# Transposing exp(C) and A by DMA instead of on TensorE, from the third batch on

## The chip, the cores and the metric

The kernel runs on one core of a Trainium2 chip. The metric is the device time of one execution in microseconds (us). Five engines work side by side, each through its own list of instructions in order: TensorE (PE; its weight loads are shown apart as PEld), VectorE (DVE), ScalarE (ACT), GpSimd (POOL) and SyncE (SP). POOL and SP also issue transfers, which 16 DMA engines carry out. Semaphores tie the lists together.

## The reference, cut to what matters

There are 8 batches of 8 heads, with 576 rows of 64 values each for q, k and v. First comes a Nystrom attention with 32 landmarks per head, then an MLP over all 4608 tokens:

```
q_lm = q.reshape(B, H, 32, 18, 64).mean(axis=3);  k_lm likewise
A = softmax(q @ k_lm.T / 8)       # 576 x 32 per head
Bm = softmax(q_lm @ k_lm.T / 8)   # 32 x 32
C = softmax(q_lm @ k.T / 8)       # 32 x 576
Z = Bm.T / (norm1(Bm) * norminf(Bm) + 1e-6)
for _ in range(6): Z = 2 * Z - Z @ Bm @ Z
x = A @ Z @ C @ v                 # heads side by side: 4608 x 512
h = x @ w_in                      # 4608 x 2048
out = (h * sigmoid(h)) @ w_out    # 4608 x 512
```

C is contracted with v over the 576 keys, so exp(C) is needed with the keys on the partitions; the scores come out of TensorE with (head, landmark) on the partitions. A comes out with the tokens on the partitions and is needed with (head, landmark) there. Both have to be transposed.

## The kernel before

Each batch passes through an attention stage and an MLP stage. The eight heads form two groups g of four, so that 4 heads by 32 landmarks fill 128 partitions.

Attention stage of a batch (class `Att`):

- `c_scores(g)` (L288) computes the scores of C for a group into a pair of PSUM banks, 128 x 576. `c_max` (L296) takes the row maximum on DVE. `c_exp(g)` (L304) is one ACT instruction with a running sum that writes a contiguous 128 x 576 bf16 tile `eC`.
- `c_transpose(g)` (L311) is six PE transposes of 128 x 96 pieces. Piece c takes every sixth column of `eC`, since v is loaded with key 6n + c at partition n. They go to one PSUM tile, `ctp`. `c_out(g)` (L317) copies it to `eCT` in SBUF: on DVE for batches 1 to 7, on ACT for batch 0.
- `w_mm(g)` (L328) multiplies `eCT` with v in 24 small matmuls (`wp`), and `w_out` (L337) scales the result by `wsc`, which `w_scale` (L322) prepares on DVE.
- `a_scores`, `a_max`, `a_shift` and `a_exp` produce exp(A) in three parts of 256, 256 and 64 tokens. `a_norm(i)` (L408) sums and inverts on DVE (L412, L413) and multiplies on POOL (L414) into `an`.
- `a_transpose(g)` (L418) is five PE transposes into the PSUM tile `atp`, `a_out(g)` (L425) a DVE copy into `AT`.
- `b_*`, `f_mm`, `f_out`, `ns_mm` and `ns_step` compute Z: a PE product (`fi`) and a DVE step (`fx`, L281) alternate six times. `x_out`, `z_mm` and `m_unit` fold Z, C v and w_in into `mb`.

MLP stage: `l1_mm` (L448) is four matmuls of `mb` with `AT` per step (`hps`) and `l1_act` (L458) the Silu on ACT. `l2_mm(n)` (L468) issues the next n matmuls with w_out (`ops`). After every 16, ACT copies the bank to `ost` (L484, three buffers) and SP issues its store (L486). `ops` has one PSUM bank; `hps` and the scores of C share two pairs of banks.

The order is written out by hand. Loop b (L570) runs 16 steps s of the MLP of batch b and puts the attention of batch b + 1 between them. With d = 0 (d = 4 in loop 0): step d+1 has the scores of B and C(0); d+2 the other scores and all exponentials, between two loads of an ACT table; d+3 `c_transpose(0)`, `f_mm`, `f_out`, `c_out(0)`; d+4 `c_transpose(1)`, `a_norm(0)`, `c_out(1)`, `w_scale`, `a_norm(1)`; d+5 `w_mm(0)`, `a_norm(2)`; d+6 `w_mm(1)`; d+7 and d+8 `a_transpose` and `a_out` of the groups. Steps d+3 to d+8 end with an `ns_mm`. The batch whose attention is worked on in loops 1 to 6 is thus batch 2 to 7; batch 0's stands ahead of the loops and batch 1's in loop 0. The lists EVEN and ODD (L489) say how many matmuls with w_out go into each step of an even or odd loop.

POOL issues all loads (L91 for q and k of batch b + 3, L98 for v of batch b + 2). SP issues the 36 stores and nothing else. Tiles wait for one another through semaphores that the framework places; tiles with one buffer (`an`, `eC`, `eCT`) are written again only when the readers before have ended.

Of the kernel before, what the change touches and what calls it, by code (L numbers as in the profile page):

```python
# [9 lines left out]
BF = mybir.dt.bfloat16  # L10
AF = mybir.ActivationFunctionType
# [24 lines left out]
def kernel(  # L36
# [9 lines left out]
    nc = tc.nc  # L46
    B, H, S, Dh = q.shape
    L = 32
    SEG = S // L
# [3 lines left out]
    sc = 1.0 / float(Dh) ** 0.5  # L53
    HF = S // 2
    VP = 96
    VC = S // VP
    TCH = [(c, min(c + 128, S)) for c in range(0, S, 128)]

    constp = ctx.enter_context(tc.tile_pool(name="constp", bufs=1))
    loadp = ctx.enter_context(tc.tile_pool(name="loadp", bufs=2))  # L60
    attp = ctx.enter_context(tc.tile_pool(name="attp", bufs=2))
# [8 lines left out]
    def mm(o, lhsT, rhs, start, stop):  # L70
        nc.tensor.matmul(out=o, lhsT=lhsT, rhs=rhs, start=start, stop=stop,  # L71
                         skip_group_check=True)
# [4 lines left out]
    def ps1(nm, dt=FP):  # L77
        return psa.tile([128, 512 if dt == FP else 1024], dt, tag="a", name=nm)
# [32 lines left out]
    for j in range(4):  # L111
        nc.gpsimd.dma_start(
            out=w_out_sb[:, 4 * j:4 * j + 4, :],
            in_=moe_w_out[512 * j:512 * j + 512, :].rearrange("(c p) m -> p c m", p=128))
# [11 lines left out]
    for i in range(2):  # L126
        z = constp.tile([128, 4, 4 * L, 2], BF, tag=f"bd{i}", name=f"bd{i}")
        nc.vector.memset(z, 0.0)
        bd_t.append(z)
    mask = constp.tile([128, 4, L], BF, tag="mask", name="mask")  # L130
    nc.vector.memset(mask, 0.0)
    for h in range(4):
        nc.vector.memset(mask[32 * h:32 * h + 32, h, :], 1.0)
    ident = constp.tile([128, 128], BF, tag="ident", name="ident")
# [43 lines left out]
    class Att:  # L178
        def __init__(self, b):
            self.b = b  # L180
            self.qkT, self.v, self.lmn = qkT_t[b], v_t[b], lmn_t[b]
            self.bd = bd_t[b % 2]
            self.lmk = attp.tile([128, 2, L, 2], BF, tag="lmk", name="lmk")
            self.csum = attp.tile([128, 2], FP, tag="csum", name="csum")
            self.eC, self.eCT, self.t = [None, None], [None, None], [None, None]
            self.s, self.sa, self.w = [None, None], [None] * 3, [None, None]
            self.fx = None

# [107 lines left out]
        def c_max(self, g):  # L296
# [4 lines left out]
            nc.vector.tensor_scalar(out=bs, in0=mx, scalar1=sc / SEG, scalar2=None, op0=OP.mult)  # L301
            self.t[g] = bs

        def c_exp(self, g):  # L304
            e = attp.tile([128, S], BF, tag=f"eC{g}", name="eC", bufs=1)
            nc.scalar.activation(out=e.rearrange("p (a n) -> p a n", a=2),  # L306
                                 in_=self.s[g][:, :, 0:HF], func=AF.Exp, scale=sc / SEG,
                                 bias=self.t[g], accum_out=self.csum[:, g:g + 1])
            self.eC[g] = e

        def c_transpose(self, g):  # L311
            self.t[g] = ps1("ctp", BF)
            for c in range(VC):
                nc.tensor.transpose(self.t[g][0:VP, 128 * c:128 * c + 128],  # L314
                                    self.eC[g].rearrange("p (n c) -> p c n", c=VC)[:, c, :], ident)

        def c_out(self, g, copy=nc.vector.tensor_copy):  # L317
            e = attp.tile([VP, VC, 128], BF, tag=f"eCT{g}", name="eCT", bufs=1)
            copy(out=e.rearrange("p c n -> p (c n)"), in_=self.t[g][0:VP, 0:VC * 128])
            self.eCT[g] = e  # L320

        def w_scale(self):  # L322
            self.wsc = attp.tile([128, 2], FP, tag="wsc", name="wsc")
# [4 lines left out]
        def w_mm(self, g):  # L328
            vv = self.v.rearrange("p h (c d) -> p h c d", d=Dh)
            self.w[g] = ps1("wp")  # L330
            for c in range(VC):
                for h in range(4):
                    mm(self.w[g][32 * h:32 * h + 32, 0:Dh],
                       self.eCT[g][:, c, 32 * h:32 * h + 32], vv[:, 4 * g + h, c, :],
                       start=(c == 0), stop=(c == VC - 1))

        def w_out(self, g):  # L337
# [70 lines left out]
        def a_norm(self, i):  # L408
            c, n, pr = self.a_dims(i)
            x = self.ex[0:pr, c:c + n, :].rearrange("p c (h l) -> p (c h) l", l=L)  # L410
            r = self.arec[0:pr, c:c + n, :].rearrange("p c h -> p (c h)")
            nc.vector.tensor_reduce(out=r, in_=x, op=OP.add, axis=AX.X)  # L412
            nc.vector.reciprocal(out=r, in_=r)  # L413
            nc.gpsimd.tensor_tensor(  # L414
                out=self.an[0:pr, c:c + n, :].rearrange("p c (h l) -> p (c h) l", l=L), in0=x,
                in1=r.unsqueeze(2).to_broadcast((pr, 8 * n, L)), op=OP.mult)

        def a_transpose(self, g):  # L418
            self.at = ps1("atp", BF)
            for (c, (c0, c1)) in enumerate(TCH):  # L420
                pr = c1 - c0
                nc.tensor.transpose(self.at[:, c0:c1], self.an[0:pr, c, 128 * g:128 * g + 128],  # L422
                                    ident[0:pr, 0:pr])

        def a_out(self, g):  # L425
            nc.vector.tensor_copy(out=self.AT[:, g, :], in_=self.at[:, 0:S])


        def m_unit(self, f):
# [69 lines left out]
    a = Att(0)  # L499
# [70 lines left out]
    for b in range(B):  # L570
        nxt = b + 1 < B
        cnt = EVEN if b % 2 == 0 else ODD
        h = {}
        a0 = a
        a = Att(b + 1) if nxt and b else None
# [9 lines left out]
        for s in range(NDC):  # L585
            if b == 0 and s < 4:
# [8 lines left out]
                else:  # L595
                    landmarks_out(1, lp, 0, 4)
                    a = Att(1)
# [113 lines left out]
        n = 4 + b % 2  # L711
# [32 lines left out]
```

## Time and profile before

| | |
|---|---|
| median of three runs | 315.83 us (314.72 to 316.62) |
| the profiled execution's own time | 316.06 us |
| its span, first to last instruction | 314.1 us, so 1.96 us lie around it |
| PE / DVE / ACT / POOL busy | 284.4 / 178.1 / 173.8 / 118.3 us |
| mean granted TensorE clock | 0.982 |
| `ctp` transposes of exp(C): 96 matmuls, mean | 290 ns each, weight loads 224 ns |
| `atp` transposes of A: 80 matmuls | 233 ns (64 of them) and 204 ns (16) each, weight loads 104 and 94 ns |

Matmuls overlap, so a mean duration of one is longer than the time by which it moves the next. The chain of work shows the time that each adds: it follows the last instruction back to what released it, and its pieces lie end to end.

### The profile page before, as it was taken

To read this page: it belongs to the slowest core of one execution; us is meant where nothing else is said; L and a number is where in the kernel's file an instruction comes from. 1 tells how busy PE (TensorE), PEld (TensorE's weight loads), DVE (VectorE), ACT (ScalarE), POOL (GpSimd) and SP (SyncE) were. 2 spreads that over 40 slices of the span, in tenths; PEclk is the share of its full clock that TensorE was granted. 3 is DMA by queue.
4 is the path that set the end of the run, shared out by engine and by line. 5 is a ranking of instruction groups with operands and counts; after the bars stand their busy time and mean duration, and the time that the engine had idled before them with its cause. 6 is when DMAs were issued, how large, how long until landed. Compare 5 with 4: busy or idle time off the path is not lost.

```text
span 314.1 us, 6108 instructions
## 1 busy us (share of the span) xinstructions
PE 284.4 (91%) x2472; PEld 164.0 (52%) x2472; DVE 178.1 (57%) x429; ACT 173.8 (55%) x337; POOL 118.3 (38%) x141
## 2 busy tenths in 40 slices
PE   2666967789999999999999999999999999999995
PEld 2453645435654665466546564466546654555442
DVE  4775788766677665756695567566676633000000
ACT  1225496448556854667467745685578546446311
POOL 7234322990397029540892079203950110100000
PEclk9999999859999999999999999999999999999999
DMA  6999997517064616055438224000600110010121
GB/s 119 209 212 206 198 212 139 77 21 154 20 104 89 137 60 111 33 97 123 78 66 146 74 56 90 33 33 35 112 33 35 61 39 36 35 67 33 57 78 67
DMA packets 18780, 28.17 MB, mean 90 GB/s; under 512 B 1345, under 2 KB 9537, under 8 KB 18753
## 3 DMA queue, kind: packets, MB, share of 16 engines
q0 software_dynamic: 13568, 18.35, 35.3%
q1 hardware_dynamic: 5184, 9.44, 8.1%
q8 instruction: 19, 0.31, 0.4%
q14 instruction: 9, 0.07, 0.1%
HBM read 36.70 MB, written 9.44 MB: 147 GB/s over the span
## 4 chain that ended last, share of the span: by engine, by line
PE 81%; DVE 9%; ACT 4%; DMA 2%; issue 2%; POOL 1%; ACTq 0%; POOLq 0%
PE ops L71 42%; PE hps L71 18%; PE sa L71 5%; PE mp L71 4%; PE ctp L314 3%; ACT ost L484 2%; DMA nat<-in_q_dram 2%; PE fi L71 2%; PE scp L71 2%; DVE qkT L142 2%; PE atp L422 2%; PE wp L71 1%; DVE cmx L298 1%; PE lmp L71 1%; DVE arec L412 1%
## 5 line engine op out<-in xcount | busy, mean ns | idle before, releaser
L71 PE MATMUL ops<-w_out_sb,gT 128*128 128x512 bf16 x576 | 147.0, 382 | 2.4 <-ACT ost L484 2.0
L460 ACT ACTIVATE gT<-hps 128x576 bf16<-128x576 f32 x128 | 82.3, 650 | 81.2 <-PE hps L71 81.0
L71 PE MATMUL hps<-AT,mb 128*128 128x288 bf16 x512 | 85.4, 293 | 0.0
L71 PEld LDWEIGHTS <-gT 128*128 128x128 bf16 x576 | 51.3, 99 | 53.3 <-issue 10.7
L71 PEld LDWEIGHTS <-mb 128*128 128x128 bf16 x512 | 48.4, 100 | 25.4 <-issue 2.5
L414 POOL TENSOR_TENSOR an<-ex,arec 128x512 bf16<-128x512 bf16 (+1 forms) x24 | 21.4, 905 | 100.1 <-DVE arec L413 91.5
L142 DVE STREAM_TRANSPOSE qkT<-nat 128x576 f32<-128x576 f32 x32 | 39.8, 1243 | 1.6 <-DMA nat<-in_k_dram 1.2
L484 ACT COPY ost<-ops 128x512 f32<-128x512 f32 x36 | 21.1, 585 | 27.4 <-PE ops L71 24.6
L439 DVE CAST mb<-mp 128x512 bf16<-128x512 f32 x32 | 22.0, 688 | 15.3 <-PE mp L71 15.3
L281 DVE SCALAR_TENSOR_TENSOR fx<-fx,fi 128x320 bf16<-128x320 bf16 (+1 forms) x48 | 20.4, 424 | 16.6 <-PE fi L71 16.6
L164 POOL TENSOR_TENSOR lma<-nat 128x1152 f32<-128x1152 bf16 x12 | 28.5, 2375 | 0.0
L440 ACT CAST mb<-mp 128x512 bf16<-128x512 f32 x32 | 18.6, 582 | 4.6 <-PE mp L71 4.6
L121 ACT ACT_TABLE_LOAD x16 | 20.5, 1283 | 1.1 <-PEq L728 0.8
L71 PE MATMUL fi<-fx 128*128 128x160 bf16 (+1 forms) x96 | 14.9, 240 | 4.8 <-DVE fx L281 3.0
L71 PEld LDWEIGHTS <-fx 128*128 128x128 bf16 x96 | 8.3, 102 | 17.7 <-DVE fx L281 7.0
L71 PE MATMUL mp<-w_in_sb,zwT 64*32 64x512 bf16 x256 | 14.9, 418 | 2.6 <-ACT mb L440 1.4
L392 DVE TENSOR_REDUCE nm<-sa 128x16 bf16<-128x512 f32 (+1 forms) x24 | 13.7, 594 | 5.3 <-PE sa L71 5.1
L71 PEld LDWEIGHTS <-ident 128*128 128x128 bf16 x168 | 10.0, 118 | 12.1 <-issue 5.0
L405 ACT ACTIVATE ex<-sa 128x512 bf16<-128x512 f32 (+1 forms) x24 | 12.5, 524 | 5.5 <-PE sa L71 5.5
L314 PEld LDWEIGHTS <-eC 128*96 128x96 bf16 x96 | 14.5, 224 | 1.5 <-issue 0.5
L314 PE MATMUL ctp<-ident,eC 128*96 128x128 bf16 x96 | 14.3, 290 | 0.4 <-ACT ex L405 0.4
L306 ACT ACTIVATE eC<-scp,cbs 128x576 bf16<-128x576 f32 x16 | 11.7, 740 | 4.4 <-DVE cbs L301 4.2
(68 smaller groups left out, 287.1 us busy)
## 6 DMA issues: line engine op xcount, KB each, us to landing
out_dram<-ost SPq DMA_DIRECT2D x36, 256.0 KB, 2.0
nat<-in_k_dram POOLq DMA_DIRECT2D x16, 288.0 KB, 6.6
nat<-in_q_dram POOLq DMA_DIRECT2D x16, 288.0 KB, 8.1
v<-in_v_dram POOLq DMA_DIRECT2D x8, 576.0 KB, 6.3
w_in_sb<-in_moe_w_in_dram POOLq DMA_DIRECT2D x4, 512.0 KB, 13.6
w_out_sb<-in_moe_w_out_dram POOLq DMA_DIRECT2D x4, 512.0 KB, 16.3
```

The source lines that it names most:

```text
L71: nc.tensor.matmul(out=o, lhsT=lhsT, rhs=rhs, start=start, stop=stop, skip_group_check=True)
L121: nc.scalar.activation(out=spare[:, 1:2], in_=spare[:, 0:1], func=func)
L142: nc.vector.transpose(out=o.rearrange("p (l t) -> p t l", t=SEG), in_=nat_t[b][:, j, :].bitcast(FP).rearrange("p (t l) -> p t l", l=L))
L164: nc.gpsimd.tensor_tensor(out=a1, in0=nat[:, :, 0:3 * w], in1=nat[:, :, 3 * w:6 * w], op=OP.add)
L281: nc.vector.scalar_tensor_tensor(out=n[:, :, lo:160], in0=self.fx[:, :, lo:160], scalar=2.0, in1=self.p.rearrange("p (g n) -> p g n", g=2) ...
L314: nc.tensor.transpose(self.t[g][0:VP, 128 * c:128 * c + 128], self.eC[g].rearrange("p (n c) -> p c n", c=VC)[:, c, :], ident)
L392: nc.vector.tensor_reduce(out=self.nm[0:pr, c:c + n, :], in_=self.sa[i][0:pr, 0:256 * n].rearrange("p (c h l) -> p c h l", h=8, l=L), op=O ...
L414: nc.gpsimd.tensor_tensor(out=self.an[0:pr, c:c + n, :].rearrange("p c (h l) -> p (c h) l", l=L), in0=x, in1=r.unsqueeze(2).to_broadcast(( ...
L439: nc.vector.tensor_copy(out=o[:, 0, :], in_=m[0])
L440: nc.scalar.copy(out=o[:, 1, :], in_=m[1])
L460: nc.scalar.activation(out=gT_t[b][:, dc, o:o + S].rearrange("p (a n) -> p a n", a=2), in_=h[:, :, 0:HF], func=AF.Silu)
L484: nc.scalar.copy(out=ost, in_=st["ps"])
```

## The change

- Two constant tiles `eC_t[g]`, 128 x 6 x 128 bf16, replace `eC`; the last 32 columns of each 128 are set to zero once at the start.
- `c_exp(g)` writes its 576 values in chunk order in all batches: ACT reads PSUM with a step of six values and writes runs of 48. The PE transposes that remain (batches 0 and 1) read contiguous pieces.
- For batches 2 to 7 `c_transpose` and `c_out` do nothing. Instead `c_exp(g)` is followed by one transposing DMA on SP's queue, from `eC_t[g]` (128 x 768) to `eCT[g]` (128 x 6 x 128).
- For batches 2 to 7 `a_transpose` and `a_out` do nothing. Instead each `a_norm` is followed by a transposing DMA on SP for each chunk of 128 tokens (64 for the last): five per batch, from `an` to `AT`.

```diff
+    eC_t = []
+    for g in range(2):
+        z = constp.tile([128, VC, 128], BF, tag=f"eC{g}", name=f"eC{g}")
+        nc.vector.memset(z[:, :, VP:128], 0.0)
+        eC_t.append(z)
...
+            self.by_dma = b >= 2
...
         def c_exp(self, g):
-            e = attp.tile([128, S], BF, tag=f"eC{g}", name="eC", bufs=1)
-            nc.scalar.activation(out=e.rearrange("p (a n) -> p a n", a=2),
-                                 in_=self.s[g][:, :, 0:HF], func=AF.Exp, scale=sc / SEG,
-                                 bias=self.t[g], accum_out=self.csum[:, g:g + 1])
-            self.eC[g] = e
+            nc.scalar.activation(
+                out=eC_t[g][:, :, 0:VP].rearrange("p c (a n) -> p a c n", a=2),
+                in_=self.s[g][:, :, 0:HF].rearrange("p a (n c) -> p a c n", c=VC), func=AF.Exp,
+                scale=sc / SEG, bias=self.t[g], accum_out=self.csum[:, g:g + 1])
+            self.eCT[g] = attp.tile([128, VC, 128], BF, tag=f"eCT{g}", name="eCT", bufs=1)
+            if self.by_dma:
+                nc.sync.dma_start(out=self.eCT[g], in_=eC_t[g].rearrange("p c n -> p (c n)"),
+                                  transpose=True)
 
         def c_transpose(self, g):
-            self.t[g] = ps1("ctp", BF)
-            for c in range(VC):
-                nc.tensor.transpose(self.t[g][0:VP, 128 * c:128 * c + 128],
-                                    self.eC[g].rearrange("p (n c) -> p c n", c=VC)[:, c, :], ident)
+            if not self.by_dma:
+                self.t[g] = ps1("ctp", BF)
+                for c in range(VC):
+                    nc.tensor.transpose(self.t[g][0:VP, 128 * c:128 * c + 128],
+                                        eC_t[g][:, c, 0:VP], ident)
 
         def c_out(self, g, copy=nc.vector.tensor_copy):
-            e = attp.tile([VP, VC, 128], BF, tag=f"eCT{g}", name="eCT", bufs=1)
-            copy(out=e.rearrange("p c n -> p (c n)"), in_=self.t[g][0:VP, 0:VC * 128])
-            self.eCT[g] = e
+            if not self.by_dma:
+                copy(out=self.eCT[g][0:VP].rearrange("p c n -> p (c n)"),
+                     in_=self.t[g][0:VP, 0:VC * 128])
...
-                       self.eCT[g][:, c, 32 * h:32 * h + 32], vv[:, 4 * g + h, c, :],
+                       self.eCT[g][0:VP, c, 32 * h:32 * h + 32], vv[:, 4 * g + h, c, :],
...
+            if self.by_dma:
+                for m in range(c, c + n):
+                    c0, c1 = TCH[m]
+                    nc.sync.dma_start(out=self.AT[:, :, c0:c1], in_=self.an[0:pr, m, :],
+                                      transpose=True)
 
         def a_transpose(self, g):
+            if self.by_dma:
+                return
             self.at = ps1("atp", BF)
...
         def a_out(self, g):
-            nc.vector.tensor_copy(out=self.AT[:, g, :], in_=self.at[:, 0:S])
+            if not self.by_dma:
+                nc.vector.tensor_copy(out=self.AT[:, g, :], in_=self.at[:, 0:S])
```

More of the change, by code (lines that the diff above doesn't have):

```diff
@@ L184, in __init__ @@
             self.csum = attp.tile([128, 2], FP, tag="csum", name="csum")
-            self.eC, self.eCT, self.t = [None, None], [None, None], [None, None]
+            self.eCT, self.t = [None, None], [None, None]
+            self.by_dma = b >= 2
             self.s, self.sa, self.w = [None, None], [None] * 3, [None, None]
```

## The prediction

> **What bounds the kernel now.** I read the page's busy times and slices first, then the chain of work, over the span and over one loop, then the order of events on each engine around what is changed, and last the DMA share there.
>
> ```profile
> PE 284.4 (91%) x2472; PEld 164.0 (52%) x2472; DVE 178.1 (57%) x429; ACT 173.8 (55%) x337; POOL 118.3 (38%) x141
> PE   2666967789999999999999999999999999999995
> PE 81%; DVE 9%; ACT 4%; DMA 2%; issue 2%; POOL 1%; ACTq 0%; POOLq 0%
> ```
>
> From the tenth slice (about 70 us) PE never pauses: what leaves PE's list there shortens the run, unless a wait fills the place. The chain through loop 3 (the MLP of batch 3 with the attention of batch 4) gives the time that each piece of PE adds:
>
> ```profile
> 146.11 0.72 PE ctp L314 x6
> 146.83 0.12 PE f L71 x2
> ...
> 147.46 0.31 PE fi L71 x2
> 147.78 0.49 PE hps L71 x4
> 148.27 0.73 PE ctp L314 x6
> ...
> 154.15 0.35 PE atp L422 x5
> ...
> 155.89 0.35 PE atp L422 x5
> ```
>
> The four groups that the change takes off PE are all on the chain: 0.72 + 0.73 + 0.35 + 0.35 us. The chain of loop 2 shows the same (0.72, 0.73, 0.35, 0.36). In order of time, the same loop:
>
> ```profile
> 141.24 0.20 ACT L306 ACTIVATION_READ_ACCUMULATOR eC<-scp,cbs 128x1 f32 x1
> 141.95 0.21 ACT L306 ACTIVATION_READ_ACCUMULATOR eC<-scp,cbs 128x1 f32 x1
> 146.15 1.17 ACT L460 ACTIVATE gT<-hps 128x576 bf16<-128x576 f32 x2
> 149.34 1.04 POOL L414 TENSOR_TENSOR an<-ex,arec 128x512 bf16<-128x512 bf16 x1 [10.98 <-DVE arec L413]
> 149.69 0.70 DVE L325 TENSOR_TENSOR wsc<-wsc,nrm 128x2 f32<-128x2 f32 x1
> 150.42 0.36 PE L71 MATMUL wp<-v,eCT 96*32 96x64 bf16 x24
> 151.68 0.11 PEld L71 LDWEIGHTS <-fx 128*128 128x128 bf16 x2 [0.43 <-DVE fx L281]
> 152.41 0.36 PE L71 MATMUL wp<-v,eCT 96*32 96x64 bf16 x24
> ```
>
> exp(C) of the groups ends at 141.44 and 142.16 and is first used by `w_mm` at 150.42 and 152.41: that gap must cover a transposing DMA. At 151.68 PE's weight load already waits for DVE.
>
> **Part 1: transposes off PE (batches 2 to 7).** 6 x (0.72 + 0.73 + 0.35 + 0.35) = 12.9 us, from the chain. The DVE copies that go with them (two `eCT` of 0.52, two `AT` of 0.46) are off the chain.
>
> **Part 2: what is late next.** Between the `fi` of step d+3 and that of d+5, DVE runs one `ns_step`, `a_norm(0)`, `c_out(1)`, `w_scale`, `a_norm(1)` and the next `ns_step`: from 147.81 to 151.62. PE is only 0.43 behind in that weight load (about 0.1 in the chain: `fi` takes 0.25 there against 0.14 elsewhere). PE loses 0.73 of work there. DVE loses `c_out(1)`, 0.49, but the `wsc` product after it ends at 150.39, when POOL's product (149.34 + 1.04) ends; that `wsc` takes 0.70 in these batches and 0.16 at its shortest, so it is held beside POOL. If it is held until POOL ends again, DVE gains nothing and PE gives back 0.73 - 0.1 = 0.63. If it slips in ahead of POOL, DVE gains about 0.9 and nothing is given back. POOL starts 0.16 after the reciprocal that both follow, the time of the `wsc` reciprocal, so held is nearer: I take 0.5 per batch, 3.0 us in all, ends 0 and 3.8. At the `fi` products of steps d+4 and d+6 to d+8 DVE is done 0.6 us or more before PE comes (154.19 against 154.88 at step d+7), which covers the 0.35 removed there.
>
> **Part 3: exponentials in chunk order.** No row has ACT reading PSUM with a step. Bounds: nothing, or 576 elements at half rate, +0.58 each (0.74 less some 0.16 of fixed time). In loops 1, 3 and 5 `hps` of step d+4 needs the banks that the Silu starting at 146.15 frees at 146.80; PE comes at 147.61, and 0.72 earlier after the change: 0.09 us later than the bank. ACT has pauses of 0.45 and 0.16 before that, so 2 x 0.58 would cost about 0.5 in each of three loops, and about 1.2 each in batches 0 and 1: 3.9 us. Nearest is the contiguous row with as many elements; I take nothing. In batches 0 and 1 the weight loads of 128x96 (224 ns, stepping by six) become contiguous, towards the 104 ns of `an`. Their 24 products add 10.4 - 6 x 1.45 = 1.7 us to the chain (3.3% of the span, less part 1's). At the pace of the A transposes (0.07 us each for 0.12) that saves 0.7; with nothing gained from layout, 0. I take 0.4. The two fills of zeros lie under the first load (DMA until 10.24 us); their nearest row, the `bd` fill, takes 0.49.
>
> **Part 4: the transposing DMAs.** The trace has none. Seven join 4.5 stores per batch on SP, at 0.33 us of issue each for the stores: 2.3 us of SP per batch, which has room in 31.8 to 35.3. Low bound of one: a 256 KB store lands in 2.0 us. High bound: the load of v, 768 pieces of 1.5 KB, as many as the 128 x 6 rows of 256 B in exp(C), lands in 6.3 us, 4.3 of them moving. The need: `w_mm(0)` moves to about 149.0 and `w_mm(1)` to 151.0, so 7.5 us after the first exponential (8.1 in even loops) and 8.8 after the second (9.4). At the low bound, one behind the other, the second lands in 4. At the high bound the second lands 9.9 after its exponential: 1.1 and 0.5 late, 5 us over six batches. The loads of q and k share the engines until about 145.5, and in loops 1 to 4 until 76, 109, 145.5 and 174:
>
> ```profile
> 140.00:142.00 2.00, 2.00 (x23) 1.21 (x21) 1.96 (x4) 2.00 (x9) 0.00 (x0) 1.00 1.10 225
> 144.00:146.00 2.00, 2.00 (x14) 1.25 (x13) 0.53 (x4) 1.98 (x3) 0.00 (x0) 1.00 0.73 200
> 146.00:148.00 2.00, 1.91 (x17) 1.35 (x16) 1.02 (x3) 1.31 (x4) 0.00 (x0) 1.00 0.02 8
> out_dram<-ost SPq DMA_DIRECT2D x36, 256.0 KB, 2.0
> v<-in_v_dram POOLq DMA_DIRECT2D x8, 576.0 KB, 6.3
> ```
>
> (Ahead of the last two columns, DMA share and GB/s, stand the engines and the clock; then follow the issues, ended by us to landing.) The slowest store took 6.4 us. Even that delay leaves the pair inside the window if each then moves like a store. exp(C) is 192 KB per DMA, less than a store's 256: I take the store's side, no stall.
>
> The five DMAs for A start when POOL ends (150.4 and 153.0) and are first read by the next loop's `hps` (167.35, some 1.7 earlier after the change): 12 us for 1152 rows, 6.5 us at v's rate. Stores queue on SP behind POOL's products through these DMAs, by about a microsecond; three `ost` buffers cover it, at one store per 7 us.
>
> The Trainium skill, "DMA: Bandwidth & Descriptors" (Latency and other measured facts), gives a transposing DMA 261 GB/s when it isn't contiguous, and about 2.0 us fixed (Anatomy of one DMA); as an estimate 2.8 us for one of exp(C), which is hidden, so the sum would stand. The same page's Rules for kernel authors speak against the change: transfers under 64 KB pay mostly overhead, and A goes in pieces of 64 and 32 KB. By five times those 2.0 us one after another A lands some 10 us after POOL, still inside the window, and the sum again stands.
>
> **The sum**, against the profiled execution's own 316.06 (span 314.1; the median of the runs is 0.23 lower): 316.06 - 12.9 + 3.0 - 0.4 = 305.8 us.
>
> **Rivals.**
>
> *Late transposes, slower.* Place: the two `w_mm` of each batch, PE waiting on DMA. It loses 1 us per batch for each us that the second DMA lands beyond 8.8 (9.4) after its exponential. The net saving is 10.3 / 6 = 1.7 per batch, so it turns slower at about 10.8. For it: v's rate (9.9), with loads on the same engines in four of six batches adding 2 to 4: 2 x 0.8 + 4 x 3.8 = 17 us, giving 323. At twice v's price the pair needs 19.2 from the first issue, 9.7 late: 305.8 + 58 = 364. Against it: as few bytes as a store, which lands in 2.0.
>
> *Late transposes, part of the gain left.* v's rate without harm from the loads: 305.8 + 5 = 311.
>
> *SP becomes the serial part.* If each transposing DMA holds SP until it has moved, seven must fit beside 4.5 stores in 31.6 us less 10: it decides from (31.6 - 10 - 1.5) / 7 = 2.9 us each. Below that only stores wait. At 4.3 us each, loops would stretch by 7 x (4.3 - 2.9) = 10 us, 365. Against it: the store's 0.33 us of issue.
>
> *ACT sets the pace.* Stepped reads at half rate: 305.8 + 3.9 = 309.7. For it: the 0.09 us of margin in odd loops. Against: the margin is 1 us or more in even loops (d+3 holds four more matmuls).
>
> *No change.* The DMAs are issued and PE's list is shorter in any case; the time could stay within 0.5% only where a stall of about 1.7 per batch cancels the saving.
>
> **How the numbers follow.** 0.5%, 1.6 us, is about what a measurement of this kernel can tell from no change. Hidden, as summed, ACT's rival included: 0.57, with its own range 301.5 (0 for part 2, 0.7 for batches 0 and 1, and 0.3% between runs) to 309.7. Partly late, to 314.2: 0.09. Cancelled, 314.3 to 317.4: 0.05. Slower to 332, by late transposes beside loads: 0.16. Beyond, by twice v's price or by SP: 0.13. Faster 0.66, same 0.05, slower 0.29. The range runs from 301.5 to 330, which leaves out the last case and a little of both ends.
>
> **What would show it.** Right: PE's share unbroken from 70 to 255 us; no `ctp` or `atp` in the chain but for batches 0 and 1; the DMAs of exp(C) landing within 7 us; PE's wait for `fx` at step d+5 grown to about 0.9. Wrong: PE or its weight loads waiting on a DMA into `eCT` ahead of `wp` or into `AT` ahead of `hps`; stores late on SP with ACT waiting for `ost`; `eC` activations well over 0.74. The prediction fails above all if a transposing DMA takes more than 5 us of its queue.

## The result and the profile after

The changed kernel takes 299.97 us (median of 4 runs, 298.71 to 300.45) against 315.27 (4 runs): a ratio of 0.950, 95% interval 0.946 to 0.955. A second comparison gave 299.81 against 315.62, 0.948 (0.944 to 0.952). The prediction was 305.8, with a range from 301.5 to 330. The direction held, and so did the removal of four groups of transposes from PE's chain; the gain was half as large again, above all because a loss of 3.0 us that the prediction counted, for a product on DVE held up beside POOL's, did not come. The profiled execution took 300.44 with a span of 298.7, so the span shrank by 15.4 us.

The page of the changed kernel first: busy times, PE by slices, the row of the exponentials, and the new issues (count, then median us from issue to landing):

```profile
PE 266.3 (89%) x2305; PEld 150.7 (50%) x2340; DVE 165.8 (55%) x407; ACT 174.2 (58%) x337; POOL 118.2 (40%) x141
PE   1766886769999999999999999999999999999994
L314 ACT ACTIVATE eC<-scp,cbs 128x576 bf16<-128x576 f32 x16 | 11.7, 741 | 4.8 <-DVE cbs L309 4.7
AT<-an SPq DMA_TRANSPOSE x30, 4.3
eCT<-eC SPq DMA_TRANSPOSE x12, 3.7
```

PE is still unbroken from about 67 us on. It is busy for 18 us less, up to 6 of which are records that this trace lacks: 2305 matmuls stand beside 2340 weight loads, and the 35 are `ops`, busy for 141.1 us and not 147.0. Reading PSUM with a step of six cost ACT nothing: 741 ns against 740. The transposing DMAs land inside their windows: the slowest of exp(C) takes 6.3 us, and the first `w_mm` comes 7.5 us after the first exponential.

The order of time in loop 3, the loop that the prediction was worked out on:

```profile
136.12 2.69 SPq L320 DMA_TRANSPOSE eCT<-eC  x2
143.03 0.11 DVE L337 RECIPROCAL wsc<-csum 128x2 f32<-128x2 f32 x1
143.17 0.16 DVE L338 TENSOR_TENSOR wsc<-wsc,nrm 128x2 f32<-128x2 f32 x1
143.25 2.72 POOL L427 TENSOR_TENSOR an<-ex,arec 128x512 bf16<-128x512 bf16 x3 [10.24 <-ACT gT L481]
143.62 0.36 PE L71 MATMUL wp<-v,eCT 96*32 96x64 bf16 x24
144.62 0.27 PEld L71 LDWEIGHTS <-fx 128*128 128x128 bf16 x2 [0.17 <-DVE fx L289]
145.50 0.36 PE L71 MATMUL wp<-v,eCT 96*32 96x64 bf16 x24
```

The DMAs of exp(C) are issued at 136.12 and are not waited for at 143.62 and 145.50. The `wsc` product starts 0.08 us before POOL's and takes 0.16; before, it started 0.35 after POOL and took 0.70. PE's wait for `fx` went from 0.43 to 0.17 where the prediction had it grow to 0.9. And the chain of the same loop, from step d+3 to step d+8:

```profile
139.47 1.29 PE ops L71 x6
140.76 0.13 PE f L71 x2
...
141.71 0.49 PE hps L71 x4
142.20 0.86 PE ops L71 x4
143.06 0.14 PE fi L71 x2
...
143.69 0.29 PE wp L71 x24
143.98 0.16 issue
144.14 0.81 PE ops L71 x3
144.95 0.14 PE fi L71 x2
...
146.76 0.49 PE hps L71 x4
147.25 0.65 PE ops L71 x3
...
148.52 0.05 issue
148.57 0.59 PE ops L71 x2
```

The four groups are gone, and 0.32 more per loop. `fi` at step d+5 takes 0.14 instead of 0.25. The three `ops` of steps d+7 and d+8, which stood behind the transposes of A, add 0.65 and 0.05 + 0.59 instead of 0.75 each. From one store copy to the same one a loop later, loop 3 went from 31.77 to 29.28, which is 2.49; 2.15 + 0.11 + 0.2 accounts for it.

Counted from the start of the first exponential of C in one batch to that in the next, the 15.4 us come from these stretches: 1.2 before that of batch 2 (73.59, now 72.38); 1.7 in loop 1; 2.5 in each of loops 2 to 5 (for example 35.25 to 32.78 and 31.77 to 29.29); 2.6 from there to the end.

### The profile page after: what moved, and what is told of

Same layout as the page of the kernel before. It is cut to its first block, busy times and chain, and to the rows that moved or that the text cites. A ratio compares the mean times of both kernels' runs of the same rounds, so it can differ in the third digit from the quotient of the medians.

```text
span 298.7 us, 5888 instructions
## 1 busy us (share of the span) xinstructions
PE 266.3 (89%) x2305; PEld 150.7 (50%) x2340; DVE 165.8 (55%) x407; ACT 174.2 (58%) x337; POOL 118.2 (40%) x141
## 4 chain that ended last, share of the span: by engine, by line
PE 79%; DVE 9%; ACT 4%; issue 3%; DMA 2%; POOL 1%; ACTq 0%; POOLq 0%
PE ops L71 43%; PE hps L71 19%; PE sa L71 5%; PE mp L71 4%; ACT ost L505 3%; PE scp L71 2%; DMA nat<-in_q_dram 2%; DVE qkT L148 2%; PE fi L71 2%; PE wp L71 1%; PE lmp L71 1%; DVE cmx L306 1%; DVE arec L425 1%; DVE fx L289 1%; DVE fx L274 1%
## 5 line engine op out<-in xcount | busy, mean ns | idle before, releaser
L71 PE MATMUL ops<-w_out_sb,gT 128*128 128x512 bf16 x541 | 141.1, 382 | 5.3 <-ACT ost L505 2.0
L71 PEld LDWEIGHTS <-gT 128*128 128x128 bf16 x576 | 52.2, 98 | 54.2 <-issue 11.3
L306 DVE TENSOR_REDUCE cmx<-scp 128x1 f32<-128x576 f32 x16 | 12.1, 755 | 4.0 <-PE scp L71 3.5
L71 PE MATMUL lmp<-nat,ident 128*128 128x64 bf16 x144 | 8.2, 229 | 6.7 <-DMA nat<-in_k_dram 5.6
```

The source lines that it names most:

```text
L306: nc.vector.tensor_reduce(out=mx, in_=self.s[g][:, :, 0:HF], op=OP.max, axis=AX.XY, negate=True)
```

## The experiments

Times are medians; ratios are to the kernel before on the same chip.

**Chunk order alone** (`e1_chunk_only`): which part of the gain needs no DMA?

```diff
-            self.by_dma = b >= 2
+            self.by_dma = False
```

> Exponentials in chunk order in all batches, all transposes on PE. Theory: part of the gain needs no DMA. In the changed kernel the six transposes of batch 1 that read contiguous pieces add 0.34 us to the chain where they added 0.73, so batches 2 to 7 would save 6 x 2 x 0.39 = 4.6 and batches 0 and 1 the 1.2 already seen; the wsc product stays held beside POOL, since the copy of eCT ahead of it remains, and may give back up to 0.3 per batch. 309.5 to 311.5. Rival, as in the prediction: layout is worth only 0.4, the rest is the DMA's: 314.5 to 315.5.

313.14 us, ratio 0.991 (0.988 to 0.994): 2.5 us of gain, more than the prediction's 0.4 and less than the theory's 4 to 6. The chain of this kernel in loop 3 shows where the rest stayed:

```profile
144.49 0.34 PE ctp L327 x6
...
145.46 0.33 PE fi L71 x2
...
145.81 0.49 DVE fx L289
146.30 0.60 DVE arec L425
...
146.93 0.25 DVE arec L426
147.18 0.41 DVE eCT L332
147.59 0.08 DVE wsc L337
...
147.69 0.70 DVE wsc L338
148.39 0.61 DVE arec L425
...
149.02 0.25 DVE arec L426
149.27 0.36 DVE fx L289
...
149.68 0.31 PE fi L71 x2
```

A group of six transposes does add 0.34 now, not 0.72. But with PE shorter, the chain leaves PE between the two `fi` products and runs through DVE: the very row of instructions that the prediction's part 2 listed, with the held `wsc` product of 0.70 and the copy of `eCT` in it. Loops 2 to 5 shrank by 0.38 or 0.39 each (31.77 to 31.38), half of the 0.77 that the two groups lost.

**Chunk order alone, `wsc` first** (`e9_chunk_wsc_first`): is it the held product?

```diff
-                    a.c_out(1)
-                    a.w_scale()
+                    a.w_scale()
+                    a.c_out(1)
```

> Chunk order alone (all transposes on PE), with w_scale moved ahead of the copy of eCT at step d+4, no DMA transposes. Theory: in the run with chunk order alone the wsc product was held (0.70) and DVE's row of instructions up to fx set the pace at step d+5, so of 0.77 per loop only 0.38 came through. With w_scale first the product starts before POOL, takes 0.16, DVE is 0.54 earlier and PE gets the rest: 6 x 0.4 to 0.5 less than chunk order alone, 310 to 311. Rival, the bank copies or ACT hold PE there: 313, no change.

308.94 us, ratio 0.977 (0.974 to 0.981), 1 us below the range expected. All eight `wsc` products take 0.16, and loops 2 to 5 take 34.37 and 30.87, 0.5 less than with chunk order alone. Moving one small instruction in the list was worth about 4 us by the medians (3.0 between the spans of the two profiled executions, 311.0 and 308.0), and it needs none of the DMAs.

**exp(C) by DMA, A on PE** (`e2_c_dma_only`). The flag of `c_exp`, `c_transpose` and `c_out` stays, that of `a_norm`, `a_transpose` and `a_out` becomes false.

```diff
-            self.by_dma = b >= 2
+            self.c_dma = b >= 2
+            self.a_dma = False
```

> Batches 2 to 7: exp(C) by DMA, A transposed on PE as before. Theory: the A transposes are on the chain, 0.70 per batch, and lengthen the matmuls around them by 0.2 (the three ops behind them take 0.75 in the chain, without them 0.65): 6 x 0.9 = 5.4 over the changed kernel, 305.4. Rival, PE has slack that other waits fill once exp(C) is gone: within 2 us of the changed kernel, 300 to 302.

305.26 us, ratio 0.966 (0.961 to 0.971). Theory: the loops take 33.70 and 30.21, 0.92 more than in the changed kernel, for the 0.70 of the transposes and the 0.2 around them.

**A by DMA, exp(C) on PE** (`e3_a_dma_only`).

```diff
+            self.c_dma = False
+            self.a_dma = b >= 2
```

> Batches 2 to 7: A by DMA, exp(C) in chunk order transposed on PE and copied by DVE. Theory: the transposes cost 2 x 0.34 per batch on the chain, and with the copy of eCT back ahead of it the wsc product is held beside POOL again, which costs PE 0.1 to 0.5 at the fi product of step d+5: 6 x (0.68 + 0.1 to 0.5) = 4.7 to 7.1 over the changed kernel, 304.7 to 307. Rival, the wsc product isn't held: 304.

307.05 us, ratio 0.972 (0.967 to 0.976): theory, at its upper end. The `wsc` product is held again (median 0.69), and the chain runs through DVE as in the run above. The kernel itself, in the same comparison:

> The changed kernel itself, beside the kernel before and the parts on one chip. All theories: about 300, ratio 0.950.

So, counted from chunk order alone (313.1), exp(C) by DMA brings 7.9, A by DMA 6.1, both together 13.3.

**A DVE instruction in place of the copy** (`e4_dve_fill`): the changed kernel, with a sum over 384 columns whose result nobody reads.

```diff
+                scr = attp.tile([128, 12], FP, tag="scr", name="scr")
+                nc.vector.tensor_reduce(
+                    out=scr, in_=self.ex[:, 0:2, :].rearrange("p c (h l) -> p (c h) l", l=L)[:, 0:12, :],
+                    op=OP.add, axis=AX.X)
...
                     a.c_out(1)
+                    a.dve_fill()
                     a.w_scale()
```

> The changed kernel with one more DVE instruction (a sum over 384 columns, about 0.5 us, result unused) where the copy of eCT stood, ahead of w_scale, in batches 2 to 7. Theory: the prediction's part 2 failed because without that copy the wsc product starts 0.06 us after the reciprocal and POOL only 0.14 after it, so it gets in first; with 0.5 us ahead of it POOL is first again, wsc takes 0.70 instead of 0.16, DVE is 1.0 later, and PE waits about 1.1 at the fi product of step d+5, 0.8 of it on the chain: 6 x 0.8 = 5 over the changed kernel, 305. Rival, wsc was short for another reason (its reciprocal takes 0.11 now, not 0.15): wsc stays at 0.16, DVE is 0.5 later, 6 x 0.3 = 2, 302.

304.83 us, ratio 0.968 (0.963 to 0.972), at the theory's 305. In order of time, loop 3:

```profile
143.09 0.49 DVE L338 TENSOR_REDUCE scr<-ex 128x12 f32<-128x384 bf16 x1
143.32 1.04 POOL L434 TENSOR_TENSOR an<-ex,arec 128x512 bf16<-128x512 bf16 x1 [10.24 <-ACT gT L488]
...
143.69 0.69 DVE L345 TENSOR_TENSOR wsc<-wsc,nrm 128x2 f32<-128x2 f32 x1
145.66 0.11 PEld L71 LDWEIGHTS <-fx 128*128 128x128 bf16 x2 [1.15 <-DVE fx L289]
```

With half a microsecond ahead of it the product meets POOL's, is held to about POOL's end (143.32 + 1.04), and PE waits 1.15. The loops take 0.82 more each. Of the 1.05 by which the product ends later than in the changed kernel (144.38 against 143.33), the sum itself explains at most 0.49. This is the state that the prediction assumed for the changed kernel.

**Late transposes, made true** (`e6_six_more`): three unused transposing DMAs of exp(C) ahead of each of the two real ones.

```diff
             if self.by_dma:
+                for i in range(3):
+                    more = attp.tile([128, VC, 128], BF, tag=f"more{g}{i}", name="more", bufs=1)
+                    nc.sync.dma_start(out=more, in_=eC_t[g].rearrange("p c n -> p (c n)"),
+                                      transpose=True)
```

> The changed kernel with three more transposing DMAs of exp(C), into unused tiles, ahead of each of the two real ones. Theory: each holds SP for 1.24 us, one behind the other, and lands some 2.5 after its hold ends; the second real one then lands 8 x 1.24 + 2.5 = 12.4 after the first issue, where w_mm of group 1 stands 9.4 (odd loops) to 10 after it: PE waits 2.4 to 3 per batch, 6 x 2.7 = 16 over the changed kernel, 316. This is the prediction's rival of late transposes, made true. If SP's hold overlaps with the next DMA (no queueing): below 302. If loads slow them further in four of six batches: 320 to 325.

348.14 us, ratio 1.104 (1.100 to 1.108). The sign is right, the price far off: 48 us over the changed kernel and not 16. From the order of time in loop 2 (SP, POOL's load of v, PE):

```profile
124.10 0.85 POOL L98 DMA_DIRECT2D v<-in_v_dram  x1
124.41 1.25 SPq L324 DMA_TRANSPOSE eCT<-eC  x1
126.39 5.87 SPq L437 DMA_TRANSPOSE AT<-an  x4
132.69 0.51 PE L71 MATMUL wp<-v,eCT 96*32 96x64 bf16 x24 [8.79 <-DMA eCT<-eC]
133.13 1.89 PE L71 MATMUL ops<-w_out_sb,gT 128*128 128x512 bf16 x4
```

The issues do queue as expected, but the last one goes out just behind the load of v and takes 8.2 us to land, where the median is 2.8. Then PE, after 8.8 us of waiting, runs at half the clock: four `ops` take 1.89 and not 1.03. Over the whole run PE waits 36.7 us for `eCT`, more than twice the 16 expected. By stretches of the same loop (PE, PEld, DVE, ACT and POOL busy, then the granted clock, DMA share, GB/s):

```profile
123.00:127.00 4.00, 0.89 (x8) 0.43 (x5) 0.74 (x3) 0.65 (x1) 3.99 (x4) 1.00 0.78 116
127.00:131.00 4.00, 0.00 (x0) 0.00 (x0) 0.00 (x0) 0.00 (x0) 3.69 (x6) 0.52 1.23 178
131.00:135.00 4.00, 2.31 (x30) 1.12 (x31) 0.00 (x0) 0.31 (x1) 3.83 (x3) 0.50 0.91 206
135.00:139.00 4.00, 4.00 (x21) 2.19 (x19) 0.97 (x2) 1.25 (x2) 0.91 (x2) 0.70 0.00 0
```

**The same with v's load later** (`e12_six_more_v_late`): what delays the last DMA, v's load or the DMAs for A?

```diff
-            if s == 7 + d // 2 and b + 2 < B:
-                load_v(b + 2)
...
                 landmarks_pool(b + 2, s - 8 - d // 2)
+            if s == 10 + d // 2 and b + 2 < B:
+                load_v(b + 2)
```

> As the run with six more transposing DMAs per batch (348), with the load of v moved three steps later, behind POOL's landmark sums. That run's second real DMA was issued 0.3 us after v's load and took 8.2 us to land where the median is 2.8. Theory: v's load delays it; without it the DMA lands 2.8 after its issue, PE waits about 3 per batch, and the granted clock dips less: 318 to 325. Rival, the five DMAs for A queued behind it delay it, whatever v does: 340 or more.

329.01 us, ratio 1.042 (1.037 to 1.046): 19 us of the 48 go with v's load, the slowest landing into `eCT` falls from 8.2 to 4.4 us, and the median landing into `AT` from 4.5 to 2.4. That is nearer to the theory than to its rival, but 4 us above the theory's range. PE's waits for `eCT` fall from 36.7 us in all to 19.1, some 3.2 per batch, as expected. What remains over the changed kernel, about 10 us (11.5 with v's load in its old place), is not shown to be the low clock after the waits alone.

**One more ahead of each** (`e11_two_more`): how much room is there? The loop above runs once instead of three times.

```diff
-                for i in range(3):
+                for i in range(1):
```

> One more transposing DMA of exp(C) ahead of each of the two real ones. Theory: SP holds 4 x 1.24 = 5 us, the second real one lands 5 + 1.6 = 6.6 to 8 us after the first exponential, ahead of w_mm at 9.4 and before the load of v starts: no stall, within 1 us of the changed kernel, 299.5 to 301. Rival, the changed kernel's DMAs land just in time: each us shows, 305 or more.

300.04 us, ratio 0.950 (0.947 to 0.954): the changed kernel's own time. Twice the transposes of exp(C) still fit.

**Both by DMA from batch 1** (`e7_both_from_1`) and **A from batch 1, exp(C) from batch 2** (`e8_a_from_1`).

```diff
-            self.by_dma = b >= 2
+            self.c_dma = b >= 1     # in e8_a_from_1: b >= 2
+            self.a_dma = b >= 1
```

> Both by DMA from batch 1 on. For it: batch 1's transposes (2 x 0.34 for exp(C), 0.4 to 0.6 twice for A) and its DVE copies of eCT (0.41) and AT leave the chain of loop 0, and wsc is not held there (0.70 to 0.16): 1 to 2.5 faster, 297.5 to 299. Against: the 16 DMA engines are over 0.9 busy with loads from 50 to 60 us, when batch 1's transposes would move; if they land as late as 8 us there, w_mm waits: 300 to 306.

301.23 us, ratio 0.956 (0.952 to 0.959). Not faster: PE waits 4.0 us for a DMA of exp(C) in loop 0, which took 9.9 to land beside the first loads.

> A by DMA from batch 1 on, exp(C) from batch 2 on. A of batch 1 is first read 10 us or more after POOL writes it, so the loads don't matter: its transposes and copies leave the chain of loop 0, 0.3 to 1 faster: 299 to 299.7. Rival: DVE, which has four wide transposes there, sets the pace, no change, 300.

298.71 us, ratio 0.948 (0.945 to 0.952): equal to the changed kernel within the intervals.

**Four matmuls ahead of `f_mm`** (`e10_a1_four_ahead`), on top of A from batch 1:

```diff
-                l2_mm(6)
+                l2_mm(4)
                 a.c_transpose(0)
...
-                l2_mm(cnt[s] - 6)
+                l2_mm(cnt[s] - 4)
```

> A by DMA from batch 1, exp(C) from batch 2, and four instead of six of the w_out matmuls ahead of f_mm at step d+3, the other two behind it, so that PE has work while DVE makes f_out (0.5 of the chain in each odd loop). If that wait goes whole: 3 x 0.5 = 1.5 below the 298.7 of the version with A from batch 1, 297.2. If hps of step d+4 then waits for its banks (ACT frees them 0.15 ahead of PE now): 3 x 0.15, 298.3.

298.11 us, ratio 0.944 (0.941 to 0.947), the lowest median of all kernels here, by 0.6% under the changed kernel; the intervals still touch. The wait for `f_out` left the chain, but odd loops gained only 0.06 to 0.26 of the 0.5: `hps` behind it stretched from 0.49 to 0.65, as the second of the two expectations had it.

## Why the prediction was right or wrong

- *Bound by PE, groups on the chain* (part 1): right. The 2.15 per loop came off whole. What was left out is the 0.2 by which the transposes of A lengthened the three `ops` behind them, 1.2 us over six batches. Both sizes, 0.75 behind `atp` and 0.65 elsewhere, stood in the chain of before:

```profile
156.25 0.75 PE ops L71 x3
157.54 0.65 PE ops L71 x3
```

- *What is late next* (part 2): this step failed, and it carries most of the miss. It took 3.0 us of loss; the runs show none, and 0.11 per loop gained: 3.7 us in all. The mechanism was right (e4 brings it back, e1 and e3 have it on the chain, e9 removes it), and so was the list of DVE instructions. The chain's row for `fi` at that step shows the 0.11, and with a loss of 0 the sum would have been 302.8. The wrong step was "POOL starts 0.16 after the reciprocal that both follow, the time of the `wsc` reciprocal, so held is nearer". A start was compared with a duration: on DVE the next reciprocal starts at 143.03, before the last one has ended (142.86 + 0.25), and takes 0.11, so the product is at 143.17 and POOL at 143.25. POOL lost the race by 0.08 us; the end "nothing is given back" was the true one. The middle of the two ends described neither. The trace of before held the answer, in two rows:

```profile
148.93 0.25 DVE L413 RECIPROCAL arec<-arec 128x16 f32<-128x16 f32 x1
149.10 0.49 DVE L319 COPY eCT<-ctp 96x768 bf16<-96x768 bf16 x1
```

The copy starts 0.08 before the reciprocal ahead of it has ended. Put the `wsc` reciprocal in the copy's place, at 149.10, and the product, which followed its start by 0.18 there (149.51 to 149.69), comes at 149.28: 0.06 before POOL's 149.34.
- *Chunk order* (part 3): ACT's cost of nothing was right. The gain was probably put too low: 0.4 predicted for batches 0 and 1, 1.2 between these two traces up to the first exponential of batch 2. The group of transposes that stands on the chain of loop 0 fell by 0.39 (0.73 to 0.34), more than the pace of the A transposes suggested. But the eight kernels here whose code is the same up to that exponential start it anywhere from 71.6 to 73.1 us, against 73.59 in the one trace of before, so how much of the 1.2 is the layout stays open; part may be where the low granted clock falls in loop 0.
- *The DMAs* (part 4): hidden, as taken. The sizes were too low, and it mattered little. The DMAs land in 2.8 to 6.3 us (exp(C)) and 2.3 to 8.2 (A), where the store's 2.0 was taken and v's 6.3 was the upper end; 7.5 was the room. Each takes 1.23 us of SP (the median), not the store's 0.33, so 8.6 per batch and not 2.3. The rival of a serial SP put its turning point at 2.9 each. e11 shows room for two more.
- *The figures of the Trainium skill*: the estimate of 2.8 us from "DMA: Bandwidth & Descriptors" (Latency and other measured facts; Anatomy of one DMA) is what the quickest DMAs of exp(C) took: 2.8 in the last two loops, where no load runs beside them, against a median of 3.7 over all. The page fits its 2.0 us of fixed time to transfers issued by GpSimd, and these go out on SP. The same page's rule that transfers under 64 KB pay mostly overhead (Rules for kernel authors) agrees in kind with what SP shows: a piece of 32 KB of A holds it for 1.16 us and one of 64 KB for 1.24, where 192 KB of exp(C) take 1.23. It cost nothing here, since A has more than 10 us.
- *Late transposes as the slower rival*: a real edge, but its price was wrong. It was put at 1 us per us of lateness. e6 paid 48 us where the DMAs held back on SP were expected to cost 16: lateness moves the DMA into v's load, which makes it later (PE's waits come to 36.7 us), and the granted clock falls to 0.50 while PE waits.
- *One loss that was not foreseen*: loop 1 gained 1.7 and not 2.5. The rows below, of the changed kernel, show the clock at half between 64 and 72 us, and the next fence the same of the kernel before.

```profile
64.00:66.00 2.00, 1.07 (x17) 0.34 (x16) 0.96 (x2) 0.78 (x2) 1.88 (x2) 0.65 0.00 0
68.00:70.00 2.00, 2.00 (x12) 1.12 (x11) 0.66 (x3) 0.22 (x1) 2.00 (x5) 0.50 0.37 44
70.00:72.00 2.00, 2.00 (x9) 0.92 (x8) 1.20 (x4) 1.97 (x4) 0.15 (x1) 0.65 1.07 195
```

```profile
64.00:66.00 2.00, 1.69 (x16) 0.31 (x16) 1.18 (x3) 0.64 (x2) 1.84 (x3) 0.51 0.00 0
68.00:70.00 2.00, 2.00 (x7) 0.76 (x5) 1.32 (x5) 0.65 (x1) 2.00 (x5) 0.50 0.26 24
70.00:72.00 2.00, 2.00 (x15) 1.29 (x14) 0.79 (x3) 0.99 (x2) 0.42 (x1) 0.79 1.05 184
```

The dip starts and ends a little later, while loop 1's work starts 1.2 earlier, so more of it falls into the dip. The profile of the same kernel in the second comparison (`r_after`) bears this out: there the clock is 0.50 already from 60 us, 0.59 from 68 to 70 and 1.00 from 70 on, and loop 1 takes 29.28, the whole gain of 2.49. So the 0.8 goes with where the dip falls in one execution, and is not a cost of the change.

The sum as it was: 12.9 for the groups, 1.2 for the `ops` behind A, 0.7 for the `fi` wait, 1.2 ahead of loop 1, less 0.8 for the clock: 15.2 of the span's 15.4, and another 0.2 outside the span. Of these, the 1.2 and the 0.8 differ from one execution to the next (1.1 and nothing in `r_after`).

## What to carry to other kernels

Where the bounding engine's work is on the chain and its replacement has room (here 7.5 us for DMAs that landed in 3.7, at most 6.3), count the removal whole, with what it does to its neighbours; then look for the second engine's list that becomes the pace once the first is shorter, since half of a gain can stay there (e1) until one small instruction is moved (e9). Where two instructions race for something within 0.1 us, give both outcomes as separate cases with their own times, and don't average them. Transfers that are hidden have an edge: past it the loss can be three times the lateness worked out beforehand (48 us here for 16), so test with added copies of the transfer how far the edge is.

## What was not expected of the hardware

- A VectorE product of two columns took 0.16 us ahead of a GpSimd product and 0.69 to 0.70 beside it, ending with it or close to it; 0.08 us of order decided which.
- A transposing DMA takes 1.23 us of issue on SP for 192 KB (median), 1.24 for mostly 64 KB pieces and 1.16 for a single 32 KB piece, against 0.33 for a store of 256 KB: over these sizes it hardly depends on the size.
- Issued right behind the load of v, a transposing DMA took 8.2 us to land; with that load moved away, at most 4.4.
- In the stall of e6 PE stood still from 123.9 us. The granted clock was 1.00 up to 127, 0.57 in the microsecond after it and 0.50 from 128. PE began again at 132.69, and the clock was 0.50 up to 137 and 1.00 only from 138: a stall of 9 us cost more than 9.
- Six transposes whose stationary operand is 96 contiguous columns add 0.34 to the chain, with a step of six elements 0.72; the weight load itself takes 133 against 224 ns (means of the same 96 loads, in `e1_chunk_only` and before).
